# Weights asked for by SP, phi of the side queries on chip, and a new unit order, in a kernel that mixes two attention branches

## The chip, the cores and the metric

The kernel runs on one core of a Trainium2 chip. The metric is the time of one execution on the device, in microseconds (us). The core has a matmul engine (TensorE, PE in the profile), VectorE (DVE), ScalarE (ACT), GpSimd (POOL) and SyncE (SP), each with its own stream of instructions that runs in order. They meet at semaphores only. DMA transfers are requested by an engine's stream (here SP, and before the change ScalarE too) and are carried out by 16 DMA engines that all requesters share.

## The reference

Two branches read the same `x` (2048 rows of 512, bf16), and a gate per row mixes them.

```python
x = A_x
g = _sigmoid((x * gate_w).sum(-1, keepdims=True))
a = _A_ref(x, A_mem0, A_Wq, A_Wk, A_Wv, A_Wo, A_seg_len)
b = _B_ref(x, B_wq, B_wk, B_wv, B_wo, B_beta)
return g * a + (1 - g) * b
```

Branch A, the main branch, runs 64 segments of 32 rows one after the other. Each segment attends over its rows and 8 memory rows, with 32 heads of width 128, and the first 8 rows of its result are the memory of the next one:

```python
for s in range(n_seg):
    xs = x[:, s * seg_len:(s + 1) * seg_len, :].copy()
    h = jnp.concatenate([mem, xs], axis=1)
    q = jnp.einsum('btd,dhe->bhte', h, Wq)
    k = jnp.einsum('btd,dhe->bhte', h, Wk)
    v = jnp.einsum('btd,dhe->bhte', h, Wv)
    scores = jnp.einsum('bhqe,bhke->bhqk', q, k) * scale
    scores = jnp.where(mask[None, None], scores, -1000000000.0)
    p = _softmax(scores, axis=-1)
    o = jnp.einsum('bhqk,bhke->bhqe', p, v)
    o = jnp.einsum('bhte,hed->btd', o, Wo)
    mem = o[:, :M, :].copy()
    outs.append(o[:, M:, :])
```

Branch B, the side branch, has 32 heads of width 16 and four blocks of 512 rows. A block's rows attend within the block, and besides read a running memory of the blocks before it, through `phi`:

```python
phi = lambda t: jnp.where(t > 0, t + 1.0, jnp.exp(t))
for s in range(N):
    ...
    logits = jnp.einsum('bhqd,bhkd->bhqk', qs, ks) * scale + mask
    p = _softmax(logits, axis=-1)
    a_dot = jnp.einsum('bhqk,bhkd->bhqd', p, vs)
    pq = phi(qs)
    num = jnp.einsum('bhld,bhde->bhle', pq, M)
    den = jnp.einsum('bhld,bhd->bhl', pq, z)[..., None] + 1e-06
    o = g * (num / den) + (1.0 - g) * a_dot
    pk = phi(ks)
    M = M + jnp.einsum('bhld,bhle->bhde', pk, vs)
    z = z + jnp.einsum('bhld->bhd', pk)
```

## The kernel before

The program is written as a list of operations with the buffers that each reads and writes. A small planner (`Prog`) puts each operation at the end of its engine's stream, in the order in which it was written, and adds the semaphore waits that the buffers ask for. So the order of the source is the order of each engine. A DMA that must wait holds back all later DMAs of its requester.

**First stage: the side projections.** `plan_loads` (line 516) requests `x`, then the three side weights of 512 KB, all through SP. `b_projections` (line 642) makes a list of small pieces for side blocks 0 to 2: `pk` (line 672) projects keys or queries of one of four head groups f, `kn` (line 712) transposes keys and applies phi, `pv` (line 696) projects values of 128 rows, `mz` (line 726) adds phi(K) times V to the running memory in PSUM. There are 16 pieces for block 0 and 17 for each of blocks 1 and 2, then the last `mz`. Keys and queries go through staging buffers `stgk0` to `stgk3`, one per f, and are stored to DRAM (`scr_kqd`). Values go through one buffer `V17` (stored to `scr_vd`), phi of the queries of blocks 1 and 2 through three buffers `stgp` (to `scr_pQd`), the running memory through `MZ16` (to `scr_mzd`). Every store is requested by SP. After every fourth piece, `build` takes one of the twelve requests for a 1 MB part of Wk, Wq and Wv, which `weight` (line 539) puts on ScalarE's stream; the pieces are n = 2, 6, ... 46.

**Second stage: the main branch with the side attention in between.** `plan_a` (line 1260) defines short units for a group of four segments, and sixteen strings `A_LIST0` to `A_LIST15` (lines 1045 to 1253) say in which order the units of group g run. In `0.K1x` the digit is the segment in its group; `K0x` to `V1y` are half passes of projections (8 matmuls each, line 1290); lower-case `k0`, `q1`, `v0` evict them; `TK`, `TQ` transpose; `S` scores, `X` exponentials, `Y` mask, `M` sums, `L` reciprocals, `N` and `n` normalise; `PV`, `PL` apply the values; `E` evicts; `W` multiplies by Wo (line 1374); `H`, `F`, `hm`, `ax` fold the result (line 1392), and write the next memory and the rows. `KL`, `QL`, `VL` (`i` ahead for group 0) are the projections of the last 8 rows of a group's segments; the values of these go to DRAM (`scr_vld`) and come back in another layout (`VL`). `wl` requests a 512 KB part of Wo. A `~` swaps ScalarE and VectorE for the evictions of that unit.

The side attention is cut into units too: `bS` (`scores`, line 913, matmul line 931), `bE` (`expo`, line 943), `bP` (`pv`, line 964), and `bT`, which runs one of the small jobs left over (`chain`, `memory`, `finish`). A job is one side block and one f, 16 in all. Its transposed queries stand in `QTj`, keys in `KTj`, values in `Vj`, phi of the queries in `pQj`, the running memory in `MZj`; all are reloaded from DRAM by `BAttn.load` (line 885) once the job before is through with them. `LateB` (line 774) projects side block 3 in the units `pj` and finishes it in `pp`: evict, store, and for queries two further units that make phi and store it. `tail_units` (line 1445) closes a group of 128 rows: `tb` multiplies the side rows, reloaded into `oTg`, by the side output weights (`brow`, line 1465), `tf` turns the main rows and writes the result.

The buffers of the first and of the second stage lie over each other. `under` and `late_home` see to it that a unit of the second stage waits for the readers of what it overwrites.

Of the kernel before, what the change touches and what calls it, by code (L numbers as in the profile page):

```python
# [257 lines left out]
def build(nc, es, A_x, A_mem0, A_Wq, A_Wk, A_Wv, A_Wo, B_wq, B_wk, B_wv, B_wo, B_beta, gate_w, out, dbg=None):  # L258
    v = NS()
# [30 lines left out]
    def alloc(stack, *specs):  # L290
        at, spans = 0, {}
        for name, shape, dt, n in specs:
# [26 lines left out]
          ("stgk", [128, 2, 512], BF16, 4), ("V17", [128, 4, HB, 17], BF16, 0), ("stgp", [128, 512], BF16, 3))  # L319
# [19 lines left out]
    dram("pQd", [NB, 4, 128, 512])  # L339
# [66 lines left out]
    for n in range(len(pieces)):  # L406
# [17 lines left out]
        if weights and n % 4 == 2:  # L424
            weights.pop(0)()
# [16 lines left out]
def plan_const(v):  # L442
# [21 lines left out]
    gp(lambda g: g.memset(v.V17[:, :, :, 16:17], 1.0), rv, "v17o", True)  # L464
# [51 lines left out]
def plan_loads(v, A_x, A_mem0, A_Wq, A_Wk, A_Wv, B_wq, B_wk, B_wv, B_wo, B_beta, gate_w):  # L516
# [125 lines left out]
def b_projections(v):  # L642
# [29 lines left out]
    def pk(sb, f, m):  # L672
# [16 lines left out]
        if sb > 0:  # L689
            i = st["p"] = st.get("p", -1) + 1  # L690
            pst = v.stgp[i % 3]
            rp = Rs("stgp%d" % (i % 3))
            phi(stage, rs, pst[:, :], [rp], "phiq%d_%d" % (sb, f), "dve",
                lambda: store("stp%d_%d" % (sb, f), v.pQd[sb, f], pst[:, :], [rp], [Rs("pQd%d_%d" % (sb, f))], "stp%d_%d" % (sb, f), "stp%d" % (i % 3)))

    def pv(sb, tt):
# [9 lines left out]
        rv = Rs("V17_%d" % tt)  # L706
        v.evac("act", v.V17[:, tt, :, 0:16].rearrange("p (e m) d -> p m e d", e=2), v.pb[bk].rearrange("p (m e d) -> p m e d", e=2, d=16), [bk], [rv], "evv%d_%d" % (sb, tt))
        store("stv%d" % sb, v.vd[sb, :, tt, :], v.V17[:, tt, :, :].rearrange("p h w -> p (h w)"), [rv, Rs("V17o")], [Rs("vd%d_%d" % (sb, tt))],
# [17 lines left out]
    def mz(sb):  # L726
# [4 lines left out]
        for f in range(4):  # L731
            bk, o = mzb[f // 2], 136 * (f % 2)

            def fm(pe, f=f, bk=bk, o=o):
                ins = None
                for tt in range(4):
                    ins = pe.matmul(v.pb[bk][:, o:o + 136], v.phK[:, tt, f * 128:(f + 1) * 128],
                                    v.V17[:, tt, :, :].rearrange("p (e f t) w -> p e f (t w)", e=2, f=4)[:, :, f, :], start=(sb == 0 and f % 2 == 0 and tt == 0), stop=True,
                                    skip_group_check=True)
                return ins  # L740
            P.op("pe", fm, reads=[Rs("phK%d" % f)] + [Rs("V17_%d" % tt) for tt in range(4)] + [Rs("V17o")],
# [32 lines left out]
class LateB:  # L774


    def __init__(self, v):
# [4 lines left out]
        self.seq = [(k, part) for k, (m, i) in enumerate(self.work) for part in range(3 if m == "Q" else 1)]  # L782
# [3 lines left out]
        self.pst = v.oTg[:, :, :].rearrange("p c t -> p (c t)")  # L786
        v.P.op("gp", lambda g: g.memset(self.vst[:, :, 16:17], 1.0), writes=[v.Rs("t1")], name="v17l")
# [42 lines left out]
    def finish(self):  # L830
        v, P, Rs = self.v, self.v.P, self.v.Rs
        if self.q >= len(self.seq):
            return
        k, part = self.seq[self.q]
# [5 lines left out]

        def store(dst, src, res, wres):
            P.dma(P.group("ls%d_%d" % (k, part), "ls" + (m if part == 0 else "P")), lambda s: s.dma_start(dst, src), reads=[Rs(res)], writes=[Rs(wres)], name="lst%d_%d" % (k, part))
        if part == 0:
            bk = self.bank.pop(k)
            dst, src, res = {"V": (self.vst[:, :, 0:16].rearrange("p (e m) d -> p m e d", e=2), v.pb[bk].rearrange("p (m e d) -> p m e d", e=2, d=16), "t1"),
                             "K": (self.kst, v.pb[bk], "aTg"), "Q": (self.qst, v.pb[bk], "adot")}[m]
            v.evac("act", dst, src, [bk], [Rs(res)], "le%d" % k)
            v.BK.give(bk)
            if m == "V":
                store(v.vd[sb, :, i, :], self.vst.rearrange("p h w -> p (h w)"), res, "vd%d_%d" % (sb, i))  # L850
            elif m == "K":
# [10 lines left out]
        if self.q == len(self.seq):  # L862
            v.wob_load()


class BAttn:
# [46 lines left out]
    def scores(self):  # L913
# [919 lines left out]
```

## Time and profile before

| what | value |
|---|---|
| median of 3 runs | 850.16 us |
| the three runs | 847.32, 850.16, 854.71 us |
| the profiled execution, whole | 852.52 us |
| its span, first to last instruction | 850.8 us |
| mean granted TensorE clock | 0.992 of full speed |
| bytes moved by DMA | 60.66 MB |

The span is what the profile sees; the whole execution has 1.7 us around it. Times in the rows below count from the start of the span. A row of a group of instructions gives the line, the engine, the operation, what is written and read, and how often. A row of waits gives who waited for whom, the total in us, the number of waits, and the longest. A row of windows gives the stretch, its length, the busy us of TensorE, of its weight loads, VectorE, ScalarE and GpSimd (with instruction counts), the granted clock, the share of the DMA engines in use, and GB/s. A row of DMA issues gives how many, the KB of each and the median us from request to landing.

### The profile page before, as it was taken

The page shows a single profiled execution, that of the slowest core. Times are in us where ns is not written, and L with a number is a line of the kernel's source. Part 1 is how long each engine was busy: PE and PEld are TensorE (multiplying, and loading weights), DVE is VectorE, ACT ScalarE, POOL GpSimd, SP SyncE. Part 2 cuts the span into 40 slices and gives each one's busy share as a digit, 9 for nine tenths or more (in the row PEclk, how much of TensorE's full clock was granted, in tenths as well). Part 3 has the DMA queues.
Part 4 walks back from the last instruction along what each step waited for, and adds up shares of the span by engine and source line. Part 5 has one row for each costly group of instructions (what it writes and reads, how often), then busy time and mean ns, then how long its engine had stood idle before and what let it go on. Part 6 is the DMA issues. An engine that isn't in the chain of part 4 may idle for free.

```text
span 850.8 us, 49479 instructions
## 1 busy us (share of the span) xinstructions
PE 814.5 (96%) x22174; PEld 435.6 (51%) x22174; DVE 579.1 (68%) x1382; ACT 586.4 (69%) x1505; POOL 284.2 (33%) x780
## 2 busy tenths in 40 slices
PE   8788999999999999999999999999999999999997
PEld 4444445555555555555555555455545555455554
DVE  3556376677667777777675776678786776777654
ACT  4556677776676667768668777776667777767655
POOL 3712223433333333333333333333233333334110
PEclk9999899999999999999999999999999999999999
DMA  9996421221101111111111121111112111110111
GB/s 314 398 363 194 137 65 43 50 60 44 45 15 52 32 45 45 39 49 39 27 39 44 38 53 39 42 45 36 36 32 52 32 44 46 45 41 4 35 47 46
DMA packets 88091, 60.66 MB, mean 71 GB/s; under 512 B 55872, under 2 KB 82760, under 8 KB 86344
## 3 DMA queue, kind: packets, MB, share of 16 engines
q1 hardware_dynamic: 86152, 44.92, 18.9%
q10 hardware_dynamic: 1728, 12.58, 3.8%
q8 instruction: 174, 2.85, 1.4%
q14 instruction: 37, 0.30, 0.1%
HBM read 38.71 MB, written 18.77 MB: 68 GB/s over the span
## 4 chain that ended last, share of the span: by engine, by line
PE 82%; ACT 6%; DMA 6%; DVE 3%; issue 1%; SPq 1%; POOL 1%; DVEq 0%; POOLq 0%; ACTq 0%
PE ps L1290 44%; PE ps L1374 16%; PE ps L1392 3%; PE ps L1610 3%; PE ps L931 3%; PE ps L982 2%; DMA scr_vd<-V 2%; DMA QTj<-scr_kqd 2%; PE ps L1465 2%; PE ps L1545 1%; PE ps L1580 1%; PE ps L823 1%; ACT PT L950 1%; PE ps L679 1%; DMA wqB<-in_B_wq_dram 1%
## 5 line engine op out<-in xcount | busy, mean ns | idle before, releaser
L956 POOL TENSOR_SCALAR_AFFINE_SELECT PT<-PT 128x128 bf16<-128x128 bf16 (+2 forms) x320 | 116.9, 365 | 217.9 <-ACT PT L950 171.3
L950 ACT ACTIVATE PT<-ps 128x512 bf16<-128x512 f32 x320 | 174.5, 604 | 14.0 <-PE ps L931 11.7
L1290 PE MATMUL ps<-Wv_sb,hT 128*32 128x512 bf16 x2048 | 138.0, 379 | 0.0
L1290 PE MATMUL ps<-Wq_sb,hT 128*32 128x512 bf16 x2048 | 135.9, 379 | 0.3
L1290 PE MATMUL ps<-Wk_sb,hT 128*32 128x512 bf16 x2048 | 135.1, 379 | 0.3
L1374 PE MATMUL ps<-Wo_sb,OT_sb 128*32 128x512 bf16 x2048 | 129.2, 383 | 0.9 <-DMA Wo_sb<-in_A_Wo_dram 0.5
L1600 POOL TENSOR_TENSOR P_sb<-P_sb,R_sb 128x64 bf16<-128x64 bf16 x128 | 49.0, 383 | 144.9 <-ACT R_sb L1590 139.1
L391 ACT ACTIVATE OT_sb<-ps 128x320 bf16<-128x320 f32 x168 | 67.5, 433 | 25.7 <-PE ps L1622 24.8
L1290 PEld LDWEIGHTS ps<-Wq_sb,hT 128*32 128x32 bf16 x2048 | 58.1, 97 | 47.3 <-ACT hT L391 2.1
L391 ACT ACTIVATE WF<-ps 128x256 f32<-128x256 f32 x114 | 38.0, 381 | 63.3 <-PE ps L1374 63.3
L1290 PEld LDWEIGHTS ps<-Wk_sb,hT 128*32 128x32 bf16 x2048 | 57.3, 97 | 47.2 <-ACT hT L391 3.6
L1302 DVE STREAM_TRANSPOSE QT_sb<-QN_sb 128x256 f32<-128x256 f32 x128 | 56.5, 441 | 25.6 <-ACT QN_sb L391 23.0
L1374 PEld LDWEIGHTS ps<-Wo_sb,OT_sb 128*32 128x32 bf16 x2048 | 48.3, 96 | 49.0 <-ACT OT_sb L391 10.1
L1302 DVE STREAM_TRANSPOSE KT_sb<-KN_sb 128x256 f32<-128x256 f32 x128 | 56.1, 440 | 22.4 <-ACT KN_sb L391 19.6
L391 ACT ACTIVATE KN_sb<-ps 128x512 bf16<-128x512 f32 x74 | 44.1, 599 | 31.2 <-PE ps L1290 30.3
L1559 ACT ACTIVATE P_sb<-ps 128x224 bf16<-128x224 f32 x128 | 45.6, 358 | 26.5 <-PE ps L1550 16.8
L391 ACT ACTIVATE QN_sb<-ps 128x512 bf16<-128x512 f32 x72 | 43.1, 600 | 28.1 <-PE ps L1290 27.9
L1290 PEld LDWEIGHTS ps<-Wv_sb,hT 128*32 128x32 bf16 x2048 | 48.6, 95 | 25.3 <-ACT QN_sb L391 0.7
L1594 DVE TENSOR_TENSOR P_sb<-P_sb,R_sb 128x160 bf16<-128x160 bf16 x128 | 42.4, 333 | 22.6 <-ACT R_sb L1590 21.3
L393 DVE CAST OT_sb<-ps 128x320 bf16<-128x320 f32 x88 | 42.0, 487 | 19.9 <-PE ps L1622 18.9
L1610 PEld LDWEIGHTS ps<-P_sb,V_sb 32*128 32x128 bf16 x2048 | 23.1, 91 | 58.1 <-DVE P_sb L1594 23.9
L393 DVE CAST V_sb<-ps 128x512 bf16<-128x512 f32 x75 | 50.9, 682 | 2.8 <-PE ps L1290 2.6
(144 smaller groups left out, 1494.5 us busy)
## 6 DMA issues: line engine op xcount, KB each, us to landing
Wk_sb<-in_A_Wk_dram ACTq DMA_DIRECT2D x4, 1024.0 KB, 8.6
Wq_sb<-in_A_Wq_dram ACTq DMA_DIRECT2D x4, 1024.0 KB, 8.2
Wv_sb<-in_A_Wv_dram ACTq DMA_DIRECT2D x4, 1024.0 KB, 7.8
Wo_sb<-in_A_Wo_dram SPq DMA_DIRECT2D x8, 512.0 KB, 5.4
scr_vld<-VNL SPq DMA_DIRECT2D x16, 256.0 KB, 2.2
VL<-scr_vld SPq DMA_DIRECT2D x64, 64.0 KB, 2.6
scr_kqd<-stgk SPq DMA_DIRECT2D x12, 256.0 KB, 10.5
Vj<-scr_vd SPq DMA_DIRECT2D x32, 68.0 KB, 2.5
```

Source lines behind the costliest of these rows:

```text
L391: P.op("act", lambda a: a.activation(dst, src, ACT.Copy), reads=[v.rbank[k] for k in bks], writes=dres, name=name)
L393: P.op("dve", lambda d: d.tensor_copy(dst, src), reads=[v.rbank[k] for k in bks], writes=dres, name=name)
L931: ins = pe.matmul(v.pb[bks[t]][:, 256 * i + o:256 * i + o + w], KT[G][r, 128 * kc:128 * (kc + 1)], QT[r, q0:q0 + w], start=True, stop=True ...
L950: P.op("act", lambda a: a.activation(pt, v.pb[bk], ACT.Exp, scale=v.SCALE_B), reads=[v.rbank[bk]], writes=[rp], name="be%d_%d" % (n, t))
L956: P.op("gp", lambda g: g.affine_select(mv, mv, [[0, len(cut)], [1, 128]], ALU.is_ge, 0.0, base=0, channel_multiplier=-1), reads=[rp], writ ...
L1290: ins = pe.matmul(pb[bk][SEG * j:SEG * (j + 1), :], lhs(c), cols(w, j) if split else w[:, 512 * j:512 * (j + 1)], start=(c == 0), stop=(c ...
L1302: P.op("dve", lambda d: d.transpose(to, src), reads=reads, writes=writes, name=name)
L1374: ins = pe.matmul(pb[bk][SEG * j:SEG * (j + 1), :], lhs(4 * k + j), Wo_sb[:, 4 * k + j, :], start=(first and k == ks[0]), stop=False, skip ...
L1559: P.op("act", lambda a: a.activation(P_sb[:, b, :], pb[bk][:, 0:224], ACT.Exp, scale=SCALE), reads=[rbank[bk]], writes=[Rs("P%d" % b), Rs( ...
L1594: P.op("dve", lambda d: d.tensor_tensor(wide(P_sb, b)[:, :, 0:L], wide(P_sb, b)[:, :, 0:L], R_sb[:, b, :].rearrange("p (i q) -> p i q", q= ...
L1600: P.op(ENG["n"], lambda d: d.tensor_tensor(left(P_sb), left(P_sb), grp04(R_sb[:, b, :]), ALU.mult), reads=[Rs("R%d" % b)], writes=[Rs("P%d ...
L1610: ins = pe.matmul(pb[bks[j]][:, L * i:L * (i + 1)], V_sb[SEG * j:SEG * (j + 1), b, i * E:(i + 1) * E], P_sb[SEG * j:SEG * (j + 1), b, LW * ...
```

## The change

- `weight` no longer names ScalarE, so all twelve weight requests are in SP's stream, after pieces 2, 5, 8, ... 35.
- `stgp`, `scr_pQd`, its stores and the loads of `pQj` go. `BAttn.phi` makes `pQj` from `QTj` on chip, for the twelve jobs of blocks 1 to 3, queued as a small job after `finish` of the job before. The next reload of `QTj` comes after it. `LateB.finish` shrinks to evict and store, with 12 `pp` units in place of 20.
- `V17` has two buffers, used in turn by the side blocks. It now lies under `t1_sb`, so the memset of ones for block 3 moves from the start into the first `pp`.
- The side rows of group g + 1 are requested right after `brow` of group g, but for the first group of each block.
- `memory` reads the values' and memory's buffer of its own half only. The last tail's result also waits for the readers of `aTg`.
- All sixteen order strings are new: the same units, with 12 more `bT` and 8 fewer `pp` in all, in another order. The start of the first:

```text
before: bS ixl pj pj bE bE iQL0x iQL0 0.K1x iQL0e~ iKL1x bE bE iKL1 bP bP iKL1e pp bS iKL0x pj 0.K1y wl wl bE
after:  ixl iKL0x iQL0x iQL0 iQL1x iQL1 iKL0 pj iKL1x iKL0e iKL1 wl 0.Q1x 0.Q1y iQL1e pj 0.K0x 0.K0y 0.q1 0.TQ1 iQL0e~ iKL1e~ bS wl bE
```

The rest of the diff, cut to its core:

```diff
-          ("stgk", [128, 2, 512], BF16, 4), ("V17", [128, 4, HB, 17], BF16, 0), ("stgp", [128, 512], BF16, 3))
+          ("stgk", [128, 2, 512], BF16, 4), ("V17", [128, 2, 4, HB, 17], BF16, 0))
...
-        if weights and n % 4 == 2:
+        if weights and n % 3 == 2:
             weights.pop(0)()
...
-              writes=[Rs(res)], name="dma_%s%d" % (res, c), eng="act")
+              writes=[Rs(res)], name="dma_%s%d" % (res, c))
...
-        if sb > 0:
-            i = st["p"] = st.get("p", -1) + 1
-            pst = v.stgp[i % 3]
-            rp = Rs("stgp%d" % (i % 3))
-            phi(stage, rs, pst[:, :], [rp], "phiq%d_%d" % (sb, f), "dve",
-                lambda: store("stp%d_%d" % (sb, f), v.pQd[sb, f], pst[:, :], [rp], [Rs("pQd%d_%d" % (sb, f))], "stp%d_%d" % (sb, f), "stp%d" % (i % 3)))
...
-        rv = Rs("V17_%d" % tt)
+        rv = Rs("V17_%d_%d" % (sb % 2, tt))
...
         if sb > 0:
-            ld(v.pQj[rows, :], v.pQd[sb, f, rows, :], [Rs("pQd%d_%d" % (sb, f))], "ldp")
             ld(v.MZj[:, G, 0:68], v.mzd[sb, :, o:o + 68], [Rs("mzd%d" % sb), Rs("KTz")], "ldm")
...
                 if G:
+                    while self.phis < job:
+                        self.run_late(1)
                     self.load(job + 1, 0, "q")
...
                 self.late.append(lambda: self.finish(sb, f))
+                if 2 < job < 15:
+                    self.late.append(lambda: self.phi(job + 1))
+
+    def phi(self, job):
+        v, P, Rs = self.v, self.v.P, self.v.Rs
+        q, p, rq, rp = v.QTj[:, :], v.pQj[:, :], Rs("jQ0"), Rs("pQj")
+        P.op("act", lambda a: a.activation(p, q, ACT.Exp), reads=[rq], writes=[rp], name="lx%d" % job)
+        P.op("dve", lambda d: d.tensor_scalar(p, p, 1.0, None, op0=ALU.min), reads=[rp], writes=[rp], name="lm%d" % job)
+        P.op("dve", lambda d: d.scalar_tensor_tensor(p, q, 0.0, p, ALU.max, ALU.add), reads=[rq, rp], writes=[rp], name="lh%d" % job)
+        self.phis = job
...
-        P.op("pe", fn, reads=[Rs("jV0"), Rs("jV1")], writes=[v.rbank[nb]], name="bN" + nm)
+        P.op("pe", fn, reads=[Rs("jV%d" % G), Rs("pQj")], writes=[v.rbank[nb]], name="bN" + nm)
...
+        if g % 4 == 0:
+            b_rows(g)
...
             P.op("pe", f_, reads=[Rs("oTg"), Rs("woB")], writes=[rbank[bb]], name="brow%d" % g)
+            if g % 4 < 3:
+                b_rows(g + 1)
```

More of the change, by code (lines that the diff above doesn't have):

```diff
@@ L863, in finish @@
+        v.evac("act", view, src, [bk], [Rs(res)], "le%d" % k)
+        v.BK.give(bk)
+        P.dma(P.group("ls%d" % k, "ls" + m), lambda s: s.dma_start(dst, out), reads=[Rs(res)], writes=[Rs(wres)], name="lst%d" % k)
+        if self.q == len(self.work):
             v.wob_load()
@@ L1443, in ol_units, with b_rows @@
         return units
+    def b_rows(g):
+        sb, q = g // 4, g % 4
+        P.dma(P.group("og%d" % g, "og"), lambda sp: sp.dma_start(oTg[:, :, :], v.oTd[sb, :, :, 128 * q:128 * (q + 1)]),
+              reads=[Rs("oTd%d_%d" % (sb, f)) for f in range(4)], writes=[Rs("oTg")], name="ldo%d" % g, scratch=True)
     def tail_units(g):
```

414 lines of the change are left out of this document (197 added, 217 removed).

## The prediction

> **What bounds the kernel now.** I read the page first, for who is busy over the whole span, then windows over stages, then TensorE's waits in the bad stages, then the timeline at each wait.
>
> ```profile
> PE 814.5 (96%) x22174; PEld 435.6 (51%) x22174; DVE 579.1 (68%) x1382; ACT 586.4 (69%) x1505; POOL 284.2 (33%) x780
> ```
>
> TensorE is busy for 814.5 of 850.8 us, and the change takes no matmul away. So only the 36 us in which TensorE stands still, and the time at a lower clock, can be won. The windows (us from the span's start; the third starts at the first fold of segment 0, the fourth and its end are the first folds of groups 3 and 13) show where these lie:
>
> ```profile
> 9.64:59.22 49.58, 42.72 (x354) 24.06 (x355) 29.67 (x66) 30.13 (x55) 19.78 (x89) 0.97 1.02 382
> 59.22:91.69 32.47, 28.53 (x540) 12.50 (x540) 14.44 (x30) 18.20 (x39) 9.06 (x24) 0.84 0.72 228
> 91.69:240.60 148.91, 143.31 (x4044) 76.45 (x4048) 101.84 (x244) 107.97 (x277) 49.08 (x134) 1.00 0.20 53
> 240.60:717.40 476.80, 468.36 (x13532) 252.42 (x13528) 345.44 (x826) 341.20 (x905) 167.18 (x431) 1.00 0.16 41
> 717.40:845.49 128.09, 124.09 (x3641) 66.59 (x3633) 84.63 (x209) 85.62 (x228) 34.86 (x88) 1.00 0.13 36
> ```
>
> After 91.69 TensorE idles 5.6 + 8.4 + 4.0 = 18.0 us in 753.8, at full clock (column PEclk 1.00): ten groups take 476.8 us, 47.7 each, of which 46.8 are busy. That stage is bound by the matmuls themselves. Before 91.69 it is otherwise: the DMA engines are full (share 1.02 in the side projections), and the clock falls. Three stretches stand at half of it:
>
> ```profile
> 38.90:42.30 3.40, 3.40 (x9) 1.21 (x8) 2.31 (x6) 2.75 (x6) 2.53 (x10) 0.50 1.01 332
> 59.40:62.80 3.40, 3.40 (x40) 1.24 (x36) 0.00 (x0) 2.58 (x5) 1.18 (x4) 0.50 1.08 355
> 83.30:90.10 6.80, 5.78 (x72) 2.04 (x64) 0.32 (x1) 3.47 (x8) 2.04 (x5) 0.50 0.95 300
> ```
>
> Half speed for 3.4, 3.4 and 6.8 us is 1.7 + 1.7 + 3.4 = 6.8 us of work lost. Each stretch follows a wait. TensorE's waits from 9.6 to 59.7, then from 59.7 to 92:
>
> ```profile
> PE ps L703 <- ACT V L391: 4.5, 1, 4.5
> PE ps L931 <- DMA QTj<-scr_kqd: 1.6, 1, 1.6
> PE ps L737 <- ACT V L391: 0.7, 1, 0.7
> ...
> PE ps L1622 <- DMA VL<-scr_vld: 1.2, 1, 1.2
> PE ps L931 <- ACT OT_sb L391: 0.6, 1, 0.6
> PE ps L1610 <- ACT OT_sb L391: 0.5, 1, 0.5
> PE ps L1392 <- ACT WF L391: 0.5, 1, 0.5
> PE ps L1374 <- DMA Wo_sb<-in_A_Wo_dram: 0.5, 1, 0.5
> ```
>
> The first is named after ScalarE, but the timeline shows what ScalarE itself waited for:
>
> ```profile
> 38.06 0.63 ACT L391 ACTIVATE V<-ps 128x512 bf16<-128x512 f32 x1 [6.08 <-DMA scr_vd<-V]
> 38.74 1.78 PE L703 MATMUL ps<-woB_sb,xT 128*128 128x512 bf16 x4 [4.53 <-ACT V L391]
> ...
> 59.22 0.51 PE L931 MATMUL ps<-QTj,KTj 32*128 32x256 bf16 x8 [1.61 <-DMA QTj<-scr_kqd]
> ```
>
> The eviction of the values of side block 1 writes V17, which the store of block 0 was still reading. And why was that store late? The DMA view from 24 to 36 us:
>
> ```profile
> q10 hardware_dynamic: 535, 3.92, 77.5%
> q1 hardware_dynamic: 951, 1.12, 25.5%
> ...
> scr_kqd<-stgk SPq DMA_DIRECT2D x3, 256.0 KB, 11.2
> scr_mzd<-MZ SPq DMA_DIRECT2D x1, 136.0 KB, 14.4
> ```
>
> Queue 10 (ScalarE's, the weights) moved 3.92 MB in 535 packets, SP's queue 1 only 1.12 MB in 951: packet for packet the weights' are six times larger, so a 256 KB store takes 11.2 us.
>
> **V17 in two buffers.** Block 1 no longer waits for block 0's store: -4.53 us, and with the wait the half clock behind it, -1.7. Block 2 takes buffer 0 again a whole block later, when even today's slow store has landed (it let ScalarE go at 38.06). The 0.7 us of L737 stays: there the last eviction itself is awaited. On the clock the Trainium skill (TensorE: Matmul & The Clock Gate, the table under Why this matters for your kernels) says to avoid idle gaps above about 3 us. Here the gap of 4.53 us agrees, the one of 1.61 does not: the clock fell at 59.4 as well. By the page alone the sum below would be 1.7 us smaller.
>
> **Weights on SP, one piece in three.** The twelve 1 MB requests come after pieces 2 to 35 instead of 2 to 46, all on queue 1. ScalarE is spared twelve issues, which hide in its idle time: 0. The weights stop taking 77% of the engines from the stores; instead each store stands behind all weights asked before it. What is ahead of the first QTj load, by sizes:
>
> ```profile
> Wk_sb<-in_A_Wk_dram ACTq DMA_DIRECT2D x4, 1024.0 KB, 8.6
> Wo_sb<-in_A_x_dram SPq DMA_DIRECT2D x8, 256.0 KB, 6.5
> scr_vd<-V SPq DMA_DIRECT2D x12, 136.0 KB, 4.9
> ...
> 0.00:16.00 16.00, 12.11 (x77) 6.20 (x78) 5.57 (x12) 6.15 (x10) 4.27 (x14) 1.00 0.87 280
> 12.00:38.00 26.00, 22.22 (x171) 12.78 (x169) 15.26 (x34) 15.61 (x29) 14.61 (x68) 1.00 1.03 404
> 49.18 1.02 PE L679 MATMUL ps<-xT,wkB 128*128 128x512 bf16 x4
> 116.71 3.45 PE ps L1290 x64
> ...
> DMA packets 3406, 7.94 MB, mean 361 GB/s; under 512 B 784, under 2 KB 2218, under 8 KB 2765
> ```
>
> x 8 x 256, three side weights of 512, weights 12 x 1024, nine stgk stores of 256, eight value stores and two MZ stores of 136, KTj and QTj 192: 19,730 KB = 20.2 MB. By 16 us 280 GB/s x 16 = 4.5 MB have moved; the other 15.7 MB at 404 GB/s take 39 us: QTj lands at 55 us, at 382 (the second window) 57, at 361 (the last row, 38 to 60 us) 59.5. TensorE ends the side projections today at 59.22 - 1.61 = 57.6; then at 57.6 - 4.53 - 1.7 = 51.3 us. Today scores stand first there; in the new order 14 half passes (8 matmuls each, 3.45/8 = 0.43 us) stand ahead of them, 6.0 us of work, so they come at 57.3. Their weights Wk and Wq are among the first 14 MB and are there by 40 us. So the wait of 1.61 and the half clock after it go, -3.3, or stay (0) at the lowest rate. New and late next: the staging buffer stgk3, wanted by the fourth K-side eviction of block 2, after the matmuls that ran at 49.2 and would now run at 49.18 - 6.2 = 43 to 44 us. Its store has 15.9 MB up to its end: 44 us at 404 GB/s, 47.6 at 361. ScalarE would wait 0 to 3.6 us there, the other evictions behind it, then TensorE; I take +1.
>
> Against the gain speaks the Trainium skill (DMA: Bandwidth & Descriptors, Issuing engines are not separate DMA queues): all queues end in the same 16 engines, and a second issuer saves only issue time. This is the first rival.
>
> **Phi on chip.** Rows of before:
>
> ```profile
> L662 ACT ACTIVATE etmp<-stgk x8: 629/630/632, 23.5 to 52.4; 128x512 bf16<-128x512 bf16 x8
> L667 DVE TENSOR_SCALAR etmp<-etmp x20: 281/293/309, 12.4 to 55.0; 128x512 bf16<-128x512 bf16 x20
> L668 DVE SCALAR_TENSOR_TENSOR stgp<-stgk,etmp x8: 691/692/773, 24.8 to 53.8; 128x512 bf16<-128x512 bf16 x8
> L859 DVE SCALAR_TENSOR_TENSOR oTg<-adot,oTg x4: 691/734/826, 114.5 to 176.3; 128x512 bf16<-128x512 bf16 x4
> ...
> QTj<-scr_kqd SPq DMA_DIRECT2D x16, 128.0 KB, 2.4
> ```
>
> Eight phis (0.63 us ScalarE, 0.29 + 0.69 VectorE) leave the first stage, where no TensorE wait hangs on them: 0. Their eight stores of 128 KB (1 MB, 2.6 us of the full engines) and twelve later ones go, as do 24 loads nobody waited for. All twelve phis now run among the attention, eight more than today: 5.0 us of ScalarE and 8.2 of VectorE, spread over twelve groups in which both are 72% busy (341 and 345 of 477). Hidden: 0; fully exposed, one after the other, 13; I take +0.5, near the hidden end: beside such work TensorE idles 8.4 of 476.8 us, 2%. Phi also waits on ScalarE for the QTj reload, with the evictions queued behind it: at most 2.4 us twelve times if it followed the request at once; but the reload is asked for at the job's last scores, and phi comes after that job's last `bP` and two or three `bT` later, so 0.
>
> **Side rows sooner.** No wait on L1465 stands in the list: 0 gained. The cost is a wait of SP, a rival below.
>
> **New order.** After 91.69 it can win at most the 18.0 us of idling and lose without bound; the ten groups now keep within the row above, so I take 0, +-3. Before that: the second window idles 32.47 - 28.53 = 3.9 us (1.2 + 0.6 + 0.5 + 0.5 + 0.5 of it in the waits shown), and the half clock from 83.3 costs 3.4. The new order puts more work ahead of the first fold, but the store and reload of the VL rows keep about as much work between them (some 20 half passes, 8.5 us, in both orders) and the last three Wo requests still stand behind that reload on SP. I take half: -3.6 (0 to -7.3).
>
> Sum: -4.5 - 1.7 - 3.3 - 3.6 + 1 + 0.5 = -11.6. A single new wait in this stage would bring a half clock of its own, 1.7 us; I count it as likely as not, +0.9: -10.7. The profiled execution took 852.5 us (span 850.8): it becomes 841.8. The median of the three runs, 850.2, is 2.4 below that execution: 840.
>
> **Rivals.** (1) The requester makes no difference: transfers are slow because the engines are full, whichever queue. Then the QTj wait and its clock stay (+3.3), stores stay late (+1 more at stgk): 844 to 845. For: share 1.02. Against: 1.12 MB beside 3.92. Chance 0.14. (2) The new order fits worse by 0.7 us a group: 15 x 0.7 = 10.5, all is given back: 850. Nothing in the trace speaks for it but that such lists are long. 0.10. (3) Slower: the reload of oTg stands on SP right behind brow of the group before, so SP stops until TensorE gets there, and KTj, VL and Vj loads stand behind it. A load late by 1.6 us costs that plus 1.7 of half clock, 3.3; 12 of the 16 groups have such a reload. From the fourth late load on (13 us) the gain is gone and the kernel is slower than before; with one in half of the twelve it is 840 + 20 = 860. Against: SP stands still long today without harm to TensorE:
>
> ```profile
> SPq L897 <- PE ps L1022: 155.3, 18, 12.0
> SPq L1496 <- DVE aTg L1494: 58.1, 13, 7.7
> ```
>
> Chance 0.08. (4) Better: the new order also halves the 18 us: 831. Chance 0.12. The forecast, 833 to 845 of its own: 0.56.
>
> **Numbers.** A measurement here cannot tell less than about 1% from nothing. Faster by over 1% means under 841.7: rival 4 and four fifths of the forecast, 0.57. Within 1%: rivals 1 and 2 and the rest, 0.35. Slower: 0.08. The range 831 to 853 leaves out rival 3 and some of the edges.
>
> **What would show it.** Right: no wait of ScalarE for the V store, no half clock near 39 and 59 us, the first fold of WF before 82 us, groups of 47 to 48 us. Wrong: a wait of a stgk eviction for its store, first scores waiting for QTj beyond 58 us, groups above 48.4, TensorE waits on DMA behind SP after 240 us.

## The result

The changed kernel takes 846.12 us (median of 16 runs, 843.29 to 847.66) beside 849.11 for the kernel before on the same chip (16 runs, 847.29 to 855.76): a ratio of 0.995, interval 0.993 to 0.997. In a second comparison, below, it took 846.40 beside 852.04, a ratio of 0.9917 (0.989 to 0.9945). It is 3 to 6 us faster; the forecast was 840, about 10 us faster. The profiled execution took 845.4 us (span 843.4) after 852.5 (span 850.8).

The page of the changed kernel first, busy time of each engine:

```profile
PE 811.5 (96%) x22174; PEld 441.1 (52%) x22174; DVE 572.0 (68%) x1381; ACT 589.8 (70%) x1506; POOL 284.8 (34%) x780
```

TensorE stands still for 843.4 - 811.5 = 31.9 us instead of 36.3, so 4.4 us were won in waits. Half clock, as the windows below show, now costs 3.4 us instead of 6.8. The sum, 7.8, is about the 7.4 by which the span shrank. All of that lies before the first fold, which starts at 83.95 us instead of 91.69; from there to the end both kernels take the same (759.4 and 759.1 us). The windows of the changed kernel, over the stretches shown of before:

```profile
9.64:59.22 49.58, 48.67 (x504) 27.22 (x505) 27.60 (x60) 28.00 (x53) 18.12 (x90) 1.00 1.02 393
59.22:91.69 32.47, 25.61 (x588) 11.44 (x581) 14.33 (x32) 18.11 (x40) 8.64 (x23) 0.89 0.67 204
91.69:240.60 148.91, 143.08 (x4050) 77.80 (x4032) 96.22 (x238) 110.64 (x279) 52.10 (x140) 1.00 0.16 43
240.60:717.40 476.80, 468.53 (x13572) 255.36 (x13564) 348.58 (x846) 351.62 (x926) 168.32 (x430) 1.00 0.15 38
...
81.80:88.60 6.80, 5.66 (x80) 2.20 (x84) 0.42 (x2) 2.43 (x6) 0.41 (x1) 0.50 0.32 79
```

The columns are as before. The first window is repaired: 48.67 of 49.58 us busy, where it was 42.72, at full clock. The second is not: idle 32.47 - 25.61 = 6.9 us, where it was 3.9. The long stage is as before, 468.53 busy after 468.36. One stretch of half clock is left, the last row; it reaches 4.7 us into group 0. TensorE's waits, from 9.64 to 59.7 us and from 59.7 to 92, those of 0.7 us and more:

```profile
PE ps L730 <- ACT V L390: 0.7, 1, 0.7
...
PE ps L1365 <- DMA Wo_sb<-in_A_Wo_dram: 3.3, 1, 3.3
PE ps L962 <- POOL PT L936: 1.0, 1, 1.0
PE ps L909 <- DVE QN_sb L392: 0.8, 1, 0.8
PE ps L1619 <- DMA VL<-scr_vld: 0.7, 1, 0.7
```

The waits for the V store and for QTj are gone, and one for Wo stands in their place. The matmuls of TensorE in the changed kernel, from the timeline (start, duration, what, and in brackets the idle time before it and its releaser):

```profile
51.11 0.61 PE L1281 MATMUL ps<-Wk_sb,xL 128*32 128x512 bf16 x8
...
57.27 0.40 PE L909 MATMUL ps<-QTj,KTj 32*128 32x256 bf16 x8
...
78.55 0.60 PE L1365 MATMUL ps<-Wo_sb,OT_sb 128*32 128x512 bf16 x8
82.41 1.04 PE L1365 MATMUL ps<-Wo_sb,OT_sb 128*32 128x512 bf16 x8 [3.26 <-DMA Wo_sb<-in_A_Wo_dram]
83.95 0.71 PE L1383 MATMUL ps<-fold,WF 128*32 128x32 f32 x32 [0.49 <-ACT WF L390]
```

The side projections end at 51.11 us and the first scores start at 57.27 with no wait in front of them. Then TensorE waits 3.26 us for a part of Wo, and the half clock of 81.8 to 88.6 sets in. Why is that part late? The same view of SP's own stream:

```profile
57.92 1.07 SPq L549 DMA_DIRECT2D Wo_sb<-in_A_Wo_dram  x2
...
62.57 2.44 SPq L549 DMA_DIRECT2D Wo_sb<-in_A_Wo_dram  x3
65.14 0.41 SPq L840 DMA_DIRECT2D scr_vd<-t_sb  x1
65.60 0.43 SPq L1316 DMA_DIRECT2D scr_vld<-VNL  x1
71.34 2.50 SPq L1321 DMA_DIRECT2D VL<-scr_vld  x4
73.88 1.71 SPq L549 DMA_DIRECT2D Wo_sb<-in_A_Wo_dram  x3
```

Three requests of 512 KB stand ahead of the store of VNL, so its reload is held until 71.34, 5.3 us after the store's issue ended at 66.03. The last three requests for Wo stand behind that reload, and only leave at 73.88.

### The profile page after: what moved, and what is told of

Read it like the earlier page. It is cut to its first block, busy times and chain, and to the rows that moved or that the text cites. A ratio compares the mean times of both kernels' runs of the same rounds, so it can differ in the third digit from the quotient of the medians.

```text
span 843.4 us, 49436 instructions
## 1 busy us (share of the span) xinstructions
PE 811.5 (96%) x22174; PEld 441.1 (52%) x22174; DVE 572.0 (68%) x1381; ACT 589.8 (70%) x1506; POOL 284.8 (34%) x780
## 4 chain that ended last, share of the span: by engine, by line
PE 85%; ACT 6%; DMA 5%; DVE 2%; issue 1%; SPq 1%; DVEq 0%; POOL 0%; ACTq 0%
PE ps L1281 46%; PE ps L1365 17%; PE ps L1383 3%; PE ps L1607 3%; PE ps L909 2%; PE ps L962 2%; DMA scr_kqd<-stgk 2%; PE ps L1460 2%; PE ps L1542 2%; PE ps L678 1%; PE ps L1577 1%; ACT R_sb L1587 1%; ACT PT L930 1%; DMA Wo_sb<-in_A_Wo_dram 1%; PE ps L813 1%
## 5 line engine op out<-in xcount | busy, mean ns | idle before, releaser
L1281 PE MATMUL ps<-Wq_sb,hT 128*32 128x512 bf16 x2048 | 138.1, 383 | 0.4
L1597 POOL TENSOR_TENSOR P_sb<-P_sb,R_sb 128x64 bf16<-128x64 bf16 x128 | 50.8, 397 | 136.9 <-ACT R_sb L1587 131.1
L1281 PEld LDWEIGHTS ps<-Wk_sb,hT 128*32 128x32 bf16 x2048 | 59.4, 97 | 45.8 <-ACT hT L390 2.6
L390 ACT ACTIVATE WF<-ps 128x256 f32<-128x256 f32 x105 | 35.2, 381 | 58.7 <-PE ps L1365 56.4
L1365 PEld LDWEIGHTS ps<-Wo_sb,OT_sb 128*32 128x32 bf16 x2048 | 48.2, 96 | 48.5 <-ACT OT_sb L390 7.5
L390 ACT ACTIVATE QN_sb<-ps 128x512 bf16<-128x512 f32 x78 | 46.9, 604 | 34.0 <-PE ps L1281 33.3
L392 DVE CAST V_sb<-ps 128x512 bf16<-128x512 f32 x76 | 51.8, 682 | 5.5 <-PE ps L1281 5.1
```

What stands on the lines that cost most here:

```text
L390: P.op("act", lambda a: a.activation(dst, src, ACT.Copy), reads=[v.rbank[k] for k in bks], writes=dres, name=name)
L392: P.op("dve", lambda d: d.tensor_copy(dst, src), reads=[v.rbank[k] for k in bks], writes=dres, name=name)
L1281: ins = pe.matmul(pb[bk][SEG * j:SEG * (j + 1), :], lhs(c), cols(w, j) if split else w[:, 512 * j:512 * (j + 1)], start=(c == 0), stop=(c ...
L1365: ins = pe.matmul(pb[bk][SEG * j:SEG * (j + 1), :], lhs(4 * k + j), Wo_sb[:, 4 * k + j, :], start=(first and k == ks[0]), stop=False, skip ...
L1597: P.op(ENG["n"], lambda d: d.tensor_tensor(left(P_sb), left(P_sb), grp04(R_sb[:, b, :]), ALU.mult), reads=[Rs("R%d" % b)], writes=[Rs("P%d ...
```

## Experiments

Ratios are to the kernel before, with a 95% interval, from runs beside it on the same chip. Group lengths are from the first fold of one group to that of the next.

**The kernel before again**, twice: how much of the picture belongs to one execution.

> The kernel before, unchanged, profiled a second time. Theory A (the first profile of before was a long execution): the wait of the value eviction for its store, 4.5 us in the first profile, and the half clocks behind it differ from execution to execution; this profile shows a span of 846 to 848 us, and the waits of TensorE before 92 us plus half-clock loss add up to 2 us or more less than the 21 us of the first. Theory B (the first profile was typical, the lost gain lies in what a profile doesn't see): the same waits to within 0.3 us and a span near 850. Ratio to before 1.000 +-0.002 by both.

> The kernel before, unchanged, profiled a third time. Theory (the wait of 1.6 us for QTj and the half clock from 59.4 us belong to some executions only, and the median execution has neither): no wait for QTj over 1 us, one or two stretches of half clock, time 849 to 853 us. Rival (they belong to most): both are there again.

Measured 851.96 us, ratio 1.0003 (0.9982 to 1.0025), and a single 849.03. The first of the two profiles has no QTj wait; the second has it, in TensorE's list of waits:

```profile
PE ps L703 <- ACT V L391: 3.5, 1, 3.5
PE ps L931 <- DMA QTj<-scr_kqd: 1.6, 1, 1.6
```

and its windows show two short stretches of half clock, the first of which begins a little after the window does:

```profile
58.60:62.00 3.40, 3.40 (x44) 1.35 (x40) 0.13 (x1) 2.58 (x5) 1.17 (x4) 0.62 1.05 345
83.30:86.70 3.40, 3.35 (x36) 1.12 (x32) 0.00 (x0) 1.96 (x4) 1.81 (x5) 0.50 1.00 308
```

So the QTj wait is there in two of three profiles. The expectation that the median execution has none fell, and of the first expectation neither theory holds whole: the span is 849.2 and the value wait 4.3 us, but QTj's is missing. The half clock differs more: it lasts 13.7 us in all in the first profile, 13.7 in the second and 6.8 in the third, and behind the value wait alone 3.4, 6.8 and none. The medians of the kernel before, in the other five comparisons, were 850.6 to 852.0 us.

**All eight Wo requests at the place of the first.**

```text
-iKL1 wl 0.Q1x ... bS wl bE ... bP wl bP ... wl bE ... wl ... wl 0.L0 wl 0.TK1 bP wl
+iKL1 wl wl wl wl wl wl wl wl 0.Q1x ...
```

> The changed kernel with all eight requests for Wo moved in the first order string to the place of the first. Theory A (order on SP: the last three parts of Wo stand behind the reload of VL, which waits for its own store): the 3.3 us wait for Wo goes and so does the half clock behind it, while the VL reload stands behind 4 MB of Wo and comes 0 to 3 us later: 1 to 6 us faster than the changed kernel, first fold at 79 to 82 us in place of 83.9. Theory B (the DMA engines are full, the order does not matter): Wo lands no earlier than 80 us, the first fold stays within 0.5 us of 83.9, time within 1 us of the changed kernel (846).

Measured 850.74 us, 0.999 (0.9974 to 1.0005): the whole gain is lost. SP's stream and ScalarE's in this run, from the timeline:

```profile
60.18 7.61 SPq L549 DMA_DIRECT2D Wo_sb<-in_A_Wo_dram  x8
67.83 9.65 SPq L840 DMA_DIRECT2D scr_vd<-t_sb  x2
...
76.49 0.62 ACT L390 ACTIVATE t_sb<-ps 128x512 bf16<-128x512 f32 x1 [9.81 <-DMA scr_vd<-t_sb]
```

TensorE's longest wait, behind it:

```profile
PE ps L962 <- POOL PT L936: 10.7, 1, 10.7
```

Four megabytes ahead of a value store of 136 KB hold ScalarE for 9.81 us, and through it TensorE for 10.7. Neither expectation has this. Asking for all of Wo at that place, on the same queue, is no cure.

**The last three Wo requests through ScalarE.**

```diff
-              writes=[Rs("Wo%d" % (q // 2))] + ([Rs("x_sb%d%d" % (q, h)) for h in range(2)] if q < 4 else []), name="dma_Wo%d" % q)
+              writes=[Rs("Wo%d" % (q // 2))] + ([Rs("x_sb%d%d" % (q, h)) for h in range(2)] if q < 4 else []), name="dma_Wo%d" % q, eng="act" if q > 4 else "sp")
```

> The changed kernel with the last three requests for Wo made by ScalarE at the same place of the order, so that they don't wait behind the reload of VL on SP. Theory A (order on SP): they are made at 65 to 68 us in place of 73.9, land by 76, no wait for Wo, no half clock: 841 to 843 us. Theory B (engines full): the store and reload of VL are slowed by as much as Wo gains, and the wait moves to VL: 845 to 847 us.

Measured 842.85 us, 0.9895 (0.9879 to 0.9911), faster than both kernels. The requests leave ScalarE from 65.91 us on. The wait for Wo is gone; a shorter one has come up, for an eviction of side block 3's values, which waits for its store, and the reload of VL leaves SP 3.9 us later than in the changed kernel. In the timelines of TensorE, ScalarE and SP:

```profile
74.87 1.05 PE L1281 MATMUL ps<-Wv_sb,xL 128*32 128x512 bf16 x16 [2.24 <-ACT t_sb L390]
84.01 0.61 PE L1383 MATMUL ps<-fold,WF 128*32 128x32 f32 x32 [0.55 <-ACT WF L390]
...
74.19 0.62 ACT L390 ACTIVATE t_sb<-ps 128x512 bf16<-128x512 f32 x1 [2.82 <-DMA scr_vd<-t_sb]
...
75.24 2.50 SPq L1321 DMA_DIRECT2D VL<-scr_vld  x4
```

No half clock follows it, nor is any left in the run. The window over that place, and the second window:

```profile
74.00:77.40 3.40, 2.53 (x52) 1.33 (x56) 2.01 (x5) 1.66 (x3) 0.00 (x0) 1.00 0.43 136
...
59.22:91.69 32.47, 25.51 (x651) 11.92 (x640) 16.00 (x37) 20.34 (x48) 10.22 (x27) 1.00 0.69 210
```

The idle time is not won: 32.47 - 25.51 = 7.0 us in the second window, as in the changed kernel, and the first fold is no sooner, 84.01 after 83.95. What is gone in this execution is the half clock: group 0, into which it reached, takes 49.9 us instead of 52.0, which is about the 2.0 us by which the span shrinks (841.4). So the wait did move, as the rival of the expectation had it, but the time is that of the theory.

**The side rows as late as before the change, alone and with the edit above**, and beside them the changed kernel once more.

```diff
-        if g % 4 == 0:
-            b_rows(g)
+        b_rows(g)
...
-            if g % 4 < 3:
-                b_rows(g + 1)
```

> The changed kernel with the reload of the side rows requested at the start of each tail, as before the change. Theory A (no TensorE wait hung on it): the same time as the changed kernel, ratio to before 0.995 +-0.001. Theory B (the early reload holds SP behind TensorE and costs): up to 3 us faster, 0.991 to 0.994. Theory C (it hides a wait): slower, 0.997 or more.

> The changed kernel once more, as the measure for the runs beside it. Theory (the last three Wo requests stand on SP behind the reload of VL, and the wait of 3.3 us with its half clock is part of the kernel): ratio to the kernel before 0.995 within 0.002, one wait of TensorE for Wo of 3 us and half clock of 6.8 us behind it. Rival (the half clock behind that wait is a matter of chance from execution to execution, as two runs of nearly the same kernel had 6.8 and 3.4 us of it): the wait is there, but half clock of 3.4 us, and a span about 1.7 us shorter than 843.4 us.

> The changed kernel with two edits: the last three Wo requests go through ScalarE, and the side rows of a group are asked for at the start of its tail, as before the change. Theory (the early request of the side rows costs nothing, and the run without it was faster only by its shorter half clock): the two edits give what the first gives alone, ratio 0.988 to 0.991. Rival (the early request holds SP and costs about 3 us by itself): the gains add up, 0.985 or less.

Late rows: 844.50 us, 0.9903 (0.9874 to 0.9933), faster than the expected 0.995. The changed kernel: 846.40, 0.9917 (0.989 to 0.9945). Both edits: 843.60, 0.9878 (0.985 to 0.9906); beside the changed kernel in the same comparison that is 2.8 us less, with all six runs (840.66 to 844.05) below all six (845.23 to 848.37), and no more than the Wo edit alone gave. So the early side rows have no cost that is clear of the noise: late rows gave 0.9903 where the changed kernel gave 0.995 in one comparison and 0.9917 in the other. A cost of up to half a per cent is not excluded. The changed kernel's second profile has the same wait for Wo, 3.2 us, but half clock for 3.4 us instead of 6.8, as the run with late rows had:

```profile
84.00:87.40 3.40, 3.37 (x60) 1.58 (x64) 0.17 (x1) 1.91 (x5) 0.41 (x1) 0.51 0.28 61
```

Its span was 843.2 us all the same: it was no sooner at the first fold (83.92), 0.7 us shorter in group 0, and lost 1.1 in group 12 (48.2 us after 47.1). Differences of 1 us between two executions are not to be read as effects here.

**One value buffer in the changed kernel**, and **its weights back on ScalarE.**

```diff
-        rv = Rs("V17_%d_%d" % (sb % 2, tt))
+        rv = Rs("V17_%d_%d" % (0, tt))
```
```diff
-              writes=[Rs(res)], name="dma_%s%d" % (res, c))
+              writes=[Rs(res)], name="dma_%s%d" % (res, c), eng="act")
```

> The changed kernel with only one of the two V17 buffers used. In the changed kernel the last value store of side block 0 is asked for at 21.4 us and lands 11.5 us later, at 33; the first value eviction of block 1 would come at 30.7. Theory A (the second buffer is what removed the wait): a wait of 2 to 3 us of ScalarE, 1 to 2 us of TensorE, 1 to 4 us slower than the changed kernel (ratio to before 0.996 to 1.000). Theory B (moving the weights to SP removed it already, since the store no longer loses against the second queue): no wait, ratio 0.995 +-0.001.

> The changed kernel with the twelve weight requests made by ScalarE, still after every third piece. Theory A (one queue in order of request is what brings QTj and the stores in time): the stores lose to the weights again, 10 us and more to landing, a TensorE wait of 2 us or more in the side projections or at the first scores, ratio to before 0.997 to 1.005. Theory B (the requester makes no difference, the engines are full either way): the same landings to within 1 us, ratio 0.995 +-0.001.

One buffer: 850.96 us, 0.9983 (0.9957 to 1.0008). ScalarE waits 2.55 us for the value store, and TensorE 2.6 behind it. Weights on ScalarE: 856.15 us, 1.0042 (1.002 to 1.0065). There VectorE and TensorE stand for a key store:

```profile
44.18 0.69 DVE L392 CAST stgk<-ps 128x512 bf16<-128x512 f32 x1 [10.11 <-DMA scr_kqd<-stgk]
44.93 0.61 PE L712 MATMUL ps<-ident,stgk 128*128 128x128 bf16 x4 [7.04 <-DVE stgk L392]
```

Against the changed kernel's 0.995 and 0.9917 the second buffer is worth 0.3 to 0.7% (its interval overlaps the first of these), and SP for the weights 0.9 to 1.3%.

**The old order with the rest of the change.** The strings of before, without the eight `pp` that have nothing left to do, and with finish and phi in one late job.

> The changed kernel with the order strings of before (without the eight units that made phi, and with phi run in the same unit as the finish of the job before it). Theory A (all of the gain is in the side projections, the new order gives nothing): about the time of the changed kernel, 845 to 848 us, though the first scores, which the old order puts first, now wait for QTj until 55 to 57 us, 4 to 6 us after the side projections end. Theory B (the new order hides that wait and is worth it): 849 to 853 us, as slow as before or slower. After the first group both expect segments of the same length to within 0.5%.

Measured 864.58 us, 1.0156 (1.0138 to 1.0174). TensorE waits 5.0 us for QTj before the first scores, and groups 2 to 13 take 47.3 to 51.4 us instead of 47.1 to 48.0. The old order has no work ahead of the first scores, and with phi where this run puts it the groups are longer.

**Phi twice, and phi for one job only.** The three operations of `phi` doubled; then `phi` returning at once for jobs 5 to 15.

> The changed kernel with the three instructions of phi run twice for each of the twelve jobs, with the same result: twelve times 0.63 us of ScalarE and 1.0 us of VectorE more. Theory A (hidden beside the matmuls): less than 2 us slower than the changed kernel, ratio to before 0.995 to 0.997. Theory B (ScalarE and VectorE are on the path in the attention groups): 8 to 20 us slower, 1.004 or more.

> The changed kernel, with phi made on chip for the side queries of job 4 alone; phi for jobs 5 to 15 is left out. Theory (the new order was written around phi, so that ScalarE and VectorE have room for it, and only more than it contains shows): groups 3 to 13 stay at 47.2 to 47.8 us, ratio within 0.003 of the changed kernel's. Rival (phi costs in this order what its doubling cost, 1.3 to 1.5 us a group in eleven groups): 15 us less, groups at 46.2, ratio 0.977. Middle: 3 to 6 us less, 0.988 to 0.991.

Doubled: 862.43 us, 1.0114 (1.0085 to 1.0144). Left out: 847.17, 0.9927 (0.99 to 0.9955), beside 0.9917 with it. The long stage, doubled and then left out:

```profile
240.60:717.40 476.80, 455.87 (x13104) 243.75 (x13099) 346.23 (x837) 346.19 (x905) 163.38 (x418) 1.00 0.15 37
```
```profile
240.60:717.40 476.80, 467.72 (x13488) 256.45 (x13472) 338.45 (x821) 345.63 (x910) 167.56 (x429) 1.00 0.15 38
```

One phi per group is hidden. A second one is not: in the same window TensorE is busy 468.53 - 455.87 = 12.7 us less, and groups 3 to 12 take 49.2 us on average instead of 47.6. These 1.6 us are what the three doubled operations take one after the other (0.63 + 0.29 + 0.69). The cover is used up.

**The kernel before with parts of the change.** The weights on SP; a ring of seven value tiles in place of four; both; both with the memset for side block 3 moved as in the change; this without phi of the queries of blocks 1 and 2; and that alone.

```diff
-              writes=[Rs(res)], name="dma_%s%d" % (res, c), eng="act")
+              writes=[Rs(res)], name="dma_%s%d" % (res, c))
...
-        rv = Rs("V17_%d" % tt)
+        tv = (4 * sb + tt) % 7
+        rv = Rs("V17_%d" % tv)
...
-            ld(v.pQj[rows, :], v.pQd[sb, f, rows, :], [Rs("pQd%d_%d" % (sb, f))], "ldp")
+            ld(v.pQj[rows, :], v.pQd[sb, f, rows, :] if sb == v.NB - 1 else v.kqd[sb, f, rows, 1, :], ...)
```

> The kernel before, with its twelve weight requests moved from ScalarE to SP, after pieces 2, 5, 8 and so on; nothing else. Theory (the requester is worth much of the first-stage gain, the second value buffer only the 2 to 3 us of the V store's wait that is left): the wait of 4.5 us for the V store shrinks to 2 to 3 us, side projections end 2 to 4 us sooner, ratio 0.995 to 0.998. Rival (the value buffer carries the gain and the requester alone is worth nothing without it): 0.999 to 1.002. Second rival (SP alone carries it all, the wait goes altogether): the scores of side block 0 some 6 us sooner, 0.991 to 0.993.

> The kernel before, with seven value tiles in a ring in place of four, so that no value eviction of block 1 waits for a late store of block 0; the weights stay on ScalarE's queue. Theory (the two edits are worth something only together: as long as the weights stand on the other queue the stores of stgk and the loads of QTj stay late, and the wait comes back in another place): the wait of 4.5 us for the V store is gone, a wait for QTj, stgk or phi of 2 us or more takes its place, ratio 0.997 to 1.001. Rival (the prediction's sum: the wait and its half clock, 6.2 us, go with the buffer alone): 0.992 to 0.994.

> The kernel before with both edits of the first stage, the ring of seven value tiles and the weights on SP; order and phi as before. Theory (the first stage's gain is theirs together, and what the new order wins before the first fold it gives back in the wait for Wo): side projections end at 51 to 53 us, ratio 0.992 to 0.995, as the whole change. Rival (the gain comes from the new order, which puts 6 us of other work ahead of the first scores): a wait for QTj of 4 us or more at the first scores, as in the run with the old order, and a ratio of 0.998 or more.

> As the run with the ring and the weights on SP, but the memset of ones into the buffer of side block 3, which in that layout lies over the value tiles and made GpSimd wait 19.9 us for their stores, is moved into the first late unit, as in the change. Theory (two things made that run slow: this memset, a wait of TensorE of 3.6 us, and the stores of phi of the queries, for which VectorE waits 10.6 us and through it TensorE 6.4): the 3.6 us go, the 6.4 stay, ratio 0.998 to 1.003. Rival (the memset was all, and with it gone the two edits give the prediction's first-stage gain): 0.990 to 0.994.

> As the run beside it, but phi of the queries of blocks 1 and 2 and its stores are left out, and the queries themselves are loaded in its place, with as many bytes. Theory (the wait for the V store and the wait for phi's store stood side by side in the first stage, so that taking only one away showed the other, and the prediction's nothing for phi was wrong): no wait for phi, side projections end at 50 to 53 us, ratio 0.988 to 0.993. Rival (phi's stores are no part of it, the old order's first stage is bound by full DMA engines): within 0.002 of the run beside it.

> The kernel before, with phi of the queries of blocks 1 and 2 and its stores left out, the queries themselves loaded in its place; four value tiles and the weights on ScalarE as before. Theory (with phi gone the V store's wait of 3.5 to 4.5 us still stands, so little is won): the wait for the V store is there, ratio 0.994 to 1.000. Rival (phi's stores alone held the stage, and the V store came late only behind them): the V wait is under 1.5 us and the ratio 0.990 or less.

| the kernel before with | us | ratio | longest waits of TensorE before 92 us |
|---|---|---|---|
| weights on SP | 853.95 | 1.0014 (0.9991 to 1.0036) | V 2.7, phi 2.0 and 2.0 |
| ring | 861.42 | 1.0112 (1.0082 to 1.0142) | phi 8.6, memset 7.6 |
| both | 856.86 | 1.0067 (1.0044 to 1.009) | phi 3.4 and 3.0, memset 3.6, Wo 2.4 |
| both, memset moved | 851.44 | 1.000 (0.9984 to 1.0015) | phi 4.0 and 1.9 |
| both, memset moved, no phi | 851.35 | 1.000 (0.9986 to 1.0013) | QTj 5.1 |
| no phi | 849.84 | 0.9974 (0.9947 to 1.0001) | V 5.2, QTj 2.6 |

No part alone gives a gain that is clear of 1, nor do all three together in the old order. Each uncovers the next wait. The ring alone with the memset moved was not run, nor the new order without the other parts. The kernel before, and then the ring alone, by VectorE's and TensorE's timelines:

```profile
39.38 0.69 DVE L668 SCALAR_TENSOR_TENSOR stgp<-stgk,etmp 128x512 bf16<-128x512 bf16 x1 [7.07 <-DMA scr_pQd<-stgp]
```
```profile
44.44 0.69 DVE L668 SCALAR_TENSOR_TENSOR stgp<-stgk,etmp 128x512 bf16<-128x512 bf16 x1 [10.52 <-DMA scr_pQd<-stgp]
...
46.13 1.89 PE L679 MATMUL ps<-xT,wqB 128*128 128x512 bf16 x4 [8.56 <-DVE phK L668]
```

In the kernel before, VectorE was already waiting 7.07 us for a store of phi. TensorE stood until 38.74 for the value store beside it, so this wait did not show in TensorE's list. With the value wait gone, phi's store holds TensorE for 8.56 us. The ring's layout also brought a wait of its own: the memset for side block 3 now lay over value tiles, and GpSimd stood 26.4 us for their stores. It cost TensorE 7.6 us with the ring alone and is no part of the change, which moves that memset. Without phi, memset moved, the third wait stands, in TensorE's timeline, and half clock around it, in the windows:

```profile
56.88 0.61 PE L927 MATMUL ps<-QTj,KTj 32*128 32x256 bf16 x8 [5.05 <-DMA QTj<-scr_kqd]
```
```profile
53.00:59.80 6.80, 2.92 (x32) 1.06 (x36) 0.72 (x1) 2.07 (x4) 1.00 (x4) 0.50 0.89 287
```

Here the side projections end at about 51.8 us (56.88 - 5.05), as in the changed kernel, and TensorE then waits for QTj; from 10 to 60 us no other wait of it is over 1.0 us. In the changed kernel the first scores start at 57.27, practically the same time, but 6 us of other work has been done by then. It is just enough: QTj's load, asked for at 46.09 us there, took 10.7 us to land.

## Why the forecast was wrong, step by step

The profiled span was forecast to shrink by 10.7 us and shrank by 7.4. The other 3 us lie between the profile and the median, below.

**New order before the first fold, -3.6: this step failed.** It took half of 3.9 us of idling and half of 3.4 us of half clock as won. Instead the idle time of the second window rose to 6.9 us, and half clock still cost 3.4. The prediction named the reason itself, that the last three Wo requests stand behind the reload of VL on SP, and then counted a gain all the same. It did not ask when they would leave. With the first stage 6.5 us shorter TensorE reaches Wo that much sooner, while the store of VNL stands behind three other requests for Wo. The edit that takes only these three requests off SP has neither the wait for Wo nor the half clock, and takes 842.85 us; with the late side rows it is 2.8 us faster in one comparison. So the order on SP is shown as the cause of that wait. It is not shown as the cause of the idling as a whole: with the edit 7.0 us of it remain, in part for a store of values and for VL, whose reload now leaves 8.2 us after the request of its store (67.02 to 75.24) instead of 5.7. What would let all transfers of this stretch land in time stays open. In the profiles the term came out at about +2.9 in place of -3.6, 6.5 us worse. Against that the 2.4 us of costs (+1, +0.5, +0.9) did not come and some 0.8 was won elsewhere, which leaves the 3.3 us by which the span misses.

**Value buffer, -4.5 and -1.7, and QTj, -3.3: these arrived.** Side projections end at 51.1 (forecast 51.3), scores start at 57.3 (57.3), and QTj kept nobody waiting, with half a us to spare at most. The sizes were those of one execution: the other two profiles of before have 6.8 us of half clock or none behind the value wait, and one has no wait for QTj. And the terms arrived only together. The buffer alone in the kernel before made it 1.1% slower, with 7.6 us of that run's waits due to the memset, and all three first-stage edits in the old order give 1.000; in the changed kernel the gain is gone with one buffer (0.9983), with the weights on ScalarE (1.0042) and with the old order (1.0156).

**Phi leaving the first stage, 0: wrong beside the buffer, harmless in the sum.** "No TensorE wait hangs on them" was read from TensorE's list, where the value wait covered it. VectorE's timeline of before has the 7.07 us. Left out of the kernel before, alone, phi gives little (0.9974); but with the value wait gone and phi kept, in the old order, TensorE waits 4.0 and 1.9 us for it. That the value buffer's term would have been lost in the new order too was not tried.

**Phi on chip later, +0.5: right.** It costs nothing that the runs can tell (0.9927 without, 0.9917 with). The mechanism has no slack: a second phi costs its whole 1.6 us a group in the profile.

**stgk, +1:** ScalarE waited 2.5 us at most for a key store, within the 0 to 3.6 given, and no wait of TensorE followed from it. **A new half clock, +0.9:** none came but the one at the wait for Wo, counted above. **Side rows sooner, 0**, and **the ten groups, 0:** as forecast; groups 2 to 13 take 47.1 to 48.0 us, after 47.1 to 48.1.

**From profile to median.** The prediction took 2.4 us off because the median of three runs lay that far under the profiled execution. Later medians of the kernel before were mostly 851 to 852, and the changed kernel's median lies 0.7 above its own profiled execution. These 3.1 us were no gain. The waits and half clocks of the sum were read from that longer execution, so what made it long was in the sum already, and the 2.4 took some of it off a second time: of the three profiles of before, the two with 13.7 us of half clock took 852.5 and 851.0 us, the one with 6.8 took 849.0. That this is all of it is not shown.

**Rivals.** That the requester makes no difference holds in the kernel before (1.0014) and not in the changed one, where SP for the weights is worth 0.9%. The Trainium skill (DMA: Bandwidth & Descriptors, Issuing engines are not separate DMA queues) says that a second issuer saves only issue time, as all run on the same 16 engines. These runs show more than issue time: with the weights on ScalarE's queue, at the same places, a key store kept VectorE waiting 10.11 us and the changed kernel took 856.15 us. But the stores are hardly sooner than in the kernel before, or later: from 10 to 52 us a key store took 10.4 us (median, 11.1 before) and a value store 12.6 (7.0 before); with the weights on ScalarE at the changed kernel's pace they took 11.0 and 17.7. So SP is better than ScalarE at the faster pace of the weights, but it does not make the stores fast. Groups 0.7 us longer, SP held by the side rows, and half of the later idling won: none was seen (from the first fold to 838.0 us TensorE idles 17.9 us, after 18.0 in a stretch of the same length).

**Open.** The span is 0.8 us shorter than -4.5 - 1.7 - 3.3 + 2.9 (the added idling) = -6.6 makes it; nothing was tried for that. Whether the wait of 2.24 us of the best version can go too was not tried.

## What to carry to other kernels

A wait in TensorE's list hides every later wait that runs beside it: before a stall is counted as won, read the lists of VectorE, ScalarE and SP over the same stretch, and look for what else is late there. When a stage gets shorter, redo the landing time of every transfer that the next stage needs, from its place in the requester's queue, for each late small store that a reload stands behind. When a request is moved ahead, look at the next milestone (here the first fold) and not only at the wait that is gone: what the request overtakes may be waited for instead. And don't subtract the distance from a profile to a median of three runs when the runs spread by 7 us.

## What was not expected of the hardware

Half clock came in stretches of 3.4, 6.8, 10.2 (the ring alone) and 13.7 us (all of Wo first), and the length of the wait before it did not decide. A wait of 1.79 us was followed by 3.4 us of half clock in the run with both the Wo and the rows edits; one of 2.24 us at the same place, in the run with the Wo edit alone, by none:

```profile
73.97 1.90 PE L1281 MATMUL ps<-Wv_sb,xL 128*32 128x512 bf16 x16 [1.79 <-ACT t_sb L390]
```
```profile
74.00:77.40 3.40, 3.40 (x36) 1.29 (x40) 2.38 (x5) 0.39 (x1) 0.00 (x0) 0.50 0.62 184
```

And the wait of about 3.2 us for Wo was followed by 6.8 us in one execution of the changed kernel and by 3.4 in another. The Trainium skill (TensorE: Matmul & The Clock Gate, Why this matters for your kernels) advises against idle gaps above about 3 us; here gaps of 1.6 to 1.8 us were followed by half clock too, so the number is no safe bound.
